# Row maxima of an attention kernel turned on TensorE in half precision instead of single

## Chip, cores and metric

The kernel runs on one core of a Trainium2 chip. The metric is the device time of one execution in microseconds; the median of several executions counts.

## What is computed

Two layers, each an attention block with a compressive memory (A) followed by a gated MLP (B), on 2048 rows of 640. Cut to what the change touches, the attention is, for each of 32 heads of 20 columns and each of 4 segments of 512 rows:

```python
x = x + A(layernorm(x))
    logits = einsum("bhqd,bhkd->bhqk", qs, ks) * scale + mask     # within a segment, causal
    p = softmax(logits, axis=-1)
    a_dot = einsum("bhqk,bhkd->bhqd", p, vs)
    a_mem = (phi(qs) @ M) / (phi(qs) @ z + 1e-6)                  # memory of the segments before
    o = g * a_mem + (1.0 - g) * a_dot
    M, z = M + phi(ks).T @ vs, z + phi(ks).sum()
x = x + B(layernorm(x))
```

The softmax needs the maximum of each row of logits; the change concerns how the kernel brings these maxima to where they are subtracted.

## The kernel before

Each layer has three phases: attention (`phase1a`), the MLP's input (`phase1b`) and its spatial product and output (`phase2`). The change lies in attention, which runs 64 **pairs** of heads (16 pairs in each of 4 segments) one after the other. Each pair takes three **steps**, numbered t; the first step of pair n has t = 3n, and `n, c = divmod(t, 3)` gives the step's number c within the pair. Numbers are held as sums of two half-precision parts, so most products are three matmuls.

A pair's scores are computed twice. `by_queries` (line 881) lays them out with queries on the partitions, two pairs ahead (LM = 2): each step writes one or two tiles of 128 queries for both heads into the PSUM tile mp, and DVE reduces them along the keys (line 899). The widths of a step, over both heads, are 1024 for c = 0, 768 and 256 for c = 1, and 512 for c = 2. The eight columns of maxima (two heads, four query tiles) go into the first columns of an SBUF tile mxs, of which there are two. `by_keys` (line 860) computes the scores again with keys on the partitions, which is the form that the product with the values needs. There the maxima have to vary along the columns, so they enter as two extra contraction rows of the query operand qk, rows 60 and 61 of each head's 64. ACT takes the exponential (line 877). The masks of both forms are small matmuls (line 845).

`maxes` (line 917) turns the maxima: a single-precision matmul of mxs with the identity writes them as rows into a PSUM tile mtp (line 922, 64 columns of weights, two passes in the profile); ACT scales it into the first half-precision part (line 924); DVE makes the remainder (line 926); two DMAs on SP's queue write the two parts into the rows of qk for both heads (line 928). They are needed by the pair's first `by_keys`, three steps after the step in which they are turned.

The PSUM tile mtp comes from a pool of a single buffer (apm, tag "ms"). It shares it with the reads of the memory (`read`, line 766, tile num, with the DVE part at lines 790 to 794), with its updates (`update`, line 799, tile mup, DVE part at line 814), and, once, with the scales of the other weights (`other_scales`). Reads and updates are issued near the end of steps with c = 1, and their DVE parts one step later.

The order of PE's instructions is written out by hand in `run` (line 977): what a step emits in turn is what PE runs in turn. A step emits `by_queries`, `by_keys`, in steps with c = 0 also `maxes`, then work postponed from earlier steps (`later`), the products with the values (`pvs`, line 930, one head at c = 2 and the other at c = 0), and then the dense work of the phase up to the mark t + 0.8 (`until`): projections of queries, keys and values (lines 665 and 725) and, late in the phase, the output projection (line 697). The updates of the memory (`half`) follow, and at last the rest up to t + 1, memory reads among it. Other engines' order follows from the program's order and a planner's estimate of when each instruction is ready. `behind(DVE)` holds an instruction back until the step's reduction has been issued. ACT splits probabilities into two parts with POOL (`cast`, lines 912 and 914). `fetch` (line 836) loads queries and keys of a pair four steps before `by_queries` needs them.

Of the kernel before, what the change touches and what calls it, by code (L numbers as in the profile page):

```python
# [8 lines left out]
F32 = mybir.dt.float32  # L9
F32R = mybir.dt.float32r  # L10
F16 = mybir.dt.float16
# [3 lines left out]
ALU = mybir.AluOpType  # L15
# [14 lines left out]
MS = 2.0 ** 14  # L30
# [184 lines left out]
def other_scales(g, stage, pool, psum, tag):  # L215

    nc = g.nc
    last = None
    for i, w in enumerate((g.wo, *g.wi, g.wu)):
        width = D if w.cols == D else w.cols // 2  # L220
        j = 0
        for k in range(w.nk):
            n = min(128, w.dram.shape[0] - 128 * k)
            for c in range(0, w.cols, width):
                t = stage.tile([128, D], F32, tag="bg", name="wmst")[:n, :width]
                nc.sync.dma_start(t, w.dram[k * 128:k * 128 + n, w.c0 + c:w.c0 + c + width])
                if last is not None:
                    nc.vector.tensor_reduce(*last, AX.X, ALU.max, apply_absolute_value=True)
                last = g.wap[:n, i, j:j + 1], t
                yield True  # L230
                j += 1
    nc.vector.tensor_reduce(*last, AX.X, ALU.max, apply_absolute_value=True)
    yield False
    nc.vector.tensor_reduce(g.wam[:, 3:7], g.wap, AX.X, ALU.max)
    pow2_scales(g, pool, psum, tag, g.wam, 3, 4)
    nc.vector.tensor_scalar(g.yw, g.pw[:, 0:1], g.pw[:, 3:4], 2.0 ** -19, ALU.mult, ALU.mult)
    nc.vector.tensor_scalar(g.sc[:, 8:10], g.pw[:, 4:6], 2.0 ** -24, None, ALU.mult)
# [322 lines left out]
DVE, ACT = mybir.EngineType.DVE, mybir.EngineType.Activation  # L560


class Attention:
# [41 lines left out]
    def setup(self, ctx):  # L605
        g, nc, tc = self.g, self.nc, self.tc
        pool = lambda n, b, **k: ctx.enter_context(tc.tile_pool(name=n, bufs=b, reuse_waits="tile", **k))
        sk, self.p3, self.pl2, self.pr = pool("ak", 1), pool("a3", 2), pool("al2", 2), pool("amr", 1)
        av, self.u4, self.u2, self.u1 = pool("av", 1), pool("au4", 4), pool("au2", 2), pool("au1", 1)
        self.e2, self.e1, ax = pool("ae2", 2), pool("ae1", 1), [pool(f"ax{i}", 1) for i in range(2)]  # L610
        self.pl1, self.bg = pool("al1", 1), pool("abg", 2)
        self.pd = pool("apd", 2, space=PSUM)
        self.px = pool("apx", 1, space=PSUM)
        self.pm = pool("apm", 1, space=PSUM)
        self.pe = pool("ape", 1, space=PSUM)
        self.po = pool("apo", 1, space=PSUM)
        self.qk = [sk.tile([128, 2, L], F16, name=f"qk{i}") for i in range(self.NQK)]
        self.vs = [p.tile([128, 4, H, 2 * DH + 1], F16, name=f"vs{i}") for i, p in enumerate((av, sk))]
        for t in self.vs:
            nc.gpsimd.memset(t[:, :, :, DH:DH + 1], 1.0)  # L620
        self.xt = [p.tile([128, 2, KD, L], F16, name=f"xt{i}") for i, p in enumerate(ax)]
        self.mxs = [sk.tile([128, 64], F32, name=f"mxs{i}") for i in range(2)]
        for t in self.mxs:
            nc.gpsimd.memset(t, 0.0)
        self.mst = [self.u1.tile([128, NU, 8, DH + 1], F32, name=f"mst{i}") for i in range(2)]

# [254 lines left out]
    def by_queries(self, m, c):  # L881

        g, nc = self.g, self.nc
        if not 0 <= m < self.N:
            return
        todo = []
        q2, k2 = self.qk[m % self.NQK][:, 0], self.qk[m % self.NQK][:, 1]
        mp = self.px.tile([128, 2, 512], F32, tag="mp", name="mp")
        mw, red = 0, []
        for i in QCH[c]:  # L890
            w = 128 * i + 128
            todo.append((mp, mw, w, q2, 60, slice(w - 128, w), k2, slice(0, w), "q", mw + w - 128))
            red.append((i, mw, w))
            mw += w
        self.emit(todo)
        if c == 0:
            self.mx[m] = self.mxs[m % 2][:, :8].rearrange("p (h t) -> p h t", h=2)
        for i, o, w in red:
            e = nc.vector.tensor_reduce(self.mx[m][:, :, i], mp[:, :, o:o + w], AX.X, ALU.max)  # L899
        self.lead.append(e)  # L900
        if c == 2:
            pass

    def cast(self, n, h):
# [9 lines left out]
            (nc.gpsimd if h == 0 or n < self.N - self.TAIL else nc.vector).tensor_tensor(PL[:, c], P[:, h, c], PH[:, c], ALU.subtract)  # L914
        self.P[n, h] = (PH, PL)

    def maxes(self, n):

        g, nc = self.g, self.nc
        del self.mx[n]  # L920
        tp = self.pm.tile([128, 512], F32, tag="ms", name="mtp")[:, :128]
        nc.tensor.matmul(tp[:64], self.mxs[n % 2], g.ident, start=True, stop=True)
        mr = self.pr.tile([8, 2, 128], F16, tag="mr", name="mr")
        nc.scalar.mul(mr[:, 0], tp[:8], -1.0 / MS)
        with self.behind(DVE):
            nc.vector.scalar_tensor_tensor(mr[:, 1], tp[:8], -1.0 / MS, mr[:, 0], ALU.mult, ALU.subtract)
        for i in range(2):
            nc.sync.dma_start(self.qk[n % self.NQK][60 + i:125 + i:64, 0].rearrange("h (t c) -> h t c", t=4), mr[:, i])

    def pvs(self, n, h, s, m, h0):  # L930
        nc = self.nc
# [45 lines left out]
    def run(self, nseg=NSEG):  # L977
        pairs = [(s, m, h0) for s in range(nseg) for m in range(NU) for h0 in UH[m][::2]]
        N = self.N = len(pairs)
# [44 lines left out]
        for s in range(nseg):  # L1024
# [4 lines left out]
            for c in seq:  # L1029
                beg = G * s - LEAD + span * acc / tot  # L1030
                if c == "v":
                    t, w = next(vt), V
# [5 lines left out]
                elif c == "p":  # L1038
                    t, w = next(pt), V
# [3 lines left out]
                else:  # L1043
                    m, w = int(c), U
# [20 lines left out]
        def background():  # L1065

            g = self.g
            yield 6
            if not g.wo.made:
                for i, _ in enumerate(other_scales(g, self.bg, self.pl1, self.pm, "ms")):  # L1070
                    yield 6 + 1.2 * i if _ else 53
            yield 54
            for j, (w, width) in enumerate(((g.wo, D), (g.wi[1], FHH))):
                w.tiles(g.top[j])
                for i, _ in enumerate(w.load(self.bg, width, "bg")):
                    yield 55 + 1.3 * (6 * j + i)

        for _ in early():
            pass
        streams = [[next(it), i, it] for i, it in enumerate((fills(), background(), dense(), reads()))]  # L1080

        def until(t):
            while streams:
                e = min(streams)
                if e[0] >= t:
                    return
                e[0] = next(e[2], None)
                if e[0] is None:
                    streams.remove(e)

        for t in range(-LEAD, END):
            self.now = t
            f, c = divmod(t + self.LF, 3)
            if c == 0 and 0 <= f + self.LM < N:
                self.fetch(f + self.LM)
            p, r = divmod(t - self.LV - 2, 3)
            if r == 0 and 0 <= p < N:
                self.combine(p, *pairs[p])
            n, c = divmod(t, 3)
            self.lead = []  # L1100
            self.by_queries(n + self.LM, c)
            self.by_keys(n, c)
            if c == 0 and 0 <= n - 1 + self.LM < N:
                self.maxes(n - 1 + self.LM)
            with self.behind(DVE):
                for f in self.later.pop(t, ()):
                    f()
            p, r = divmod(t - self.LV - 0, 3)
            if r == 0 and 0 <= p < N:
                for _ in self.pvs(p, 0, *pairs[p]):  # L1110
                    pass
            p, r = divmod(t - self.LV - 0, 3)
            if r == 0 and 0 <= p + 1 < N:
                with self.behind(ACT):
                    self.cast(p + 1, 0)
            p, r = divmod(t - self.LV - 1, 3)
            if r == 0 and 0 <= p < N:
                for _ in self.pvs(p, 1, *pairs[p]):
                    pass
            p, r = divmod(t - self.LV - 1, 3)  # L1120
            if r == 0 and 0 <= p + 1 < N:
                with self.behind(ACT):
                    self.cast(p + 1, 1)
            with self.behind(DVE):
                until(t + .8)
            for f in self.half.pop(t, ()):
                f()
            with self.behind(DVE):
                until(t + 1)
        assert not self.half  # L1130
# [73 lines left out]
```

## Time and profile before

| | us |
|---|---|
| median of three runs | 2349.11 (2349.03 to 2351.12) |
| the profiled execution | 2352.33 |
| its span, first to last instruction | 2350.6 |

Mean granted TensorE clock over the span: 0.985 of full speed. In the profile PE is TensorE's matmuls and PEld its weight loads, DVE is VectorE, ACT ScalarE, POOL GpSimd, SP the queue that issues the DMAs. A name such as L899 is line 899 of the kernel, `out<-in` are the tiles that an instruction writes and reads, and `<-` behind an idle time names what ended it.

### The profile page before, as it was taken

The numbers are of one execution on the slowest core, as the hardware profiler recorded it, in microseconds if no ns is written. First come the engines' busy times: TensorE is split into PE (matmuls) and PEld (weight loads), VectorE is DVE, ScalarE is ACT, GpSimd is POOL, SyncE is SP. The second block draws the span as 40 slices with busy tenths as digits, with TensorE's granted clock in tenths as the row PEclk, the third lists the DMA queues.
The fourth block names the chain that finished last, engine by engine and source line by source line (L and its number), as shares of the span: only waits on it lengthen the run. The fifth ranks groups of instructions, "written<-read, shape, count | busy, mean of one in ns | idle before, by whom it ended". The sixth has DMA issues, their size and how long they took to land. (4 is left out here: it accounts for less than half of the span.)

```text
span 2350.6 us, 53268 instructions
## 1 busy us (share of the span) xinstructions
PE 2207.0 (94%) x21834; PEld 1321.6 (56%) x21834; DVE 1391.3 (59%) x2705; ACT 1160.5 (49%) x1440; POOL 984.5 (42%) x980
## 2 busy tenths in 40 slices
PE   5898898999999989999988999989989999999998
PEld 3455555666555545555555556556665555555554
DVE  7788877777545545444327787777764544444331
ACT  4688788888522321111127988878872322112110
POOL 2487888999411000000015888899981100000000
PEclk9999899999999999999999999999999999999999
DMA  6665654345643697775534363453464338766661
GB/s 171 153 175 146 160 156 117 88 126 131 187 113 94 170 264 164 174 173 145 131 89 109 104 139 85 109 117 95 119 172 109 94 103 213 171 175 151 161 140 50
DMA packets 504884, 325.59 MB, mean 139 GB/s; under 512 B 410672, under 2 KB 445616, under 8 KB 499520
## 3 DMA queue, kind: packets, MB, share of 16 engines
q1 hardware_dynamic: 504640, 322.20, 53.9%
q8 instruction: 171, 2.80, 0.5%
q14 instruction: 73, 0.60, 0.1%
HBM read 148.42 MB, written 85.61 MB: 100 GB/s over the span
## 5 line engine op out<-in xcount | busy, mean ns | idle before, releaser
L914 POOL TENSOR_TENSOR PL<-P,PH 128x640 f16<-128x640 f32 x504 | 705.7, 1421 | 113.6 <-ACT PH L912 97.8
L899 DVE TENSOR_REDUCE mxs<-mp 128x2 f32<-128x1024 f32 (+3 forms) x512 | 409.0, 819 | 203.1 <-PE mp L845 199.5
L424 PE MATMUL gp<-zh,wt 128*128 128x432 f16 x2048 | 465.1, 347 | 9.5 <-DMA wt<-wn 9.5
L424 PEld LDWEIGHTS <-wt 128*128 128x128 f16 x3072 | 301.4, 98 | 270.1 <-DMA wt<-wn 10.4
L877 ACT ACTIVATE P<-es,sc 128x1024 f32<-128x1024 f32 (+1 forms) x384 | 370.9, 966 | 124.0 <-PE es L845 119.7
L912 ACT CAST PH<-P 128x1280 f16<-128x1280 f32 x256 | 320.0, 1250 | 10.4 <-PE pv L942 2.6
L439 POOL MEMSET un<- 128x64 f16 x32 | 5.0, 155 | 680.9 <-DMA ut<-un 656.2
L341 PEld LDWEIGHTS <-th 128*128 128x128 f16 x1920 | 187.8, 98 | 166.6 <-issue 3.8
L424 PE MATMUL gp<-zl,wt 128*128 128x432 f16 x1024 | 272.2, 348 | 0.0
L252 POOL TENSOR_TENSOR lnrs<-lnve,mhalf 128x1 f32<-128x1 f32 x96 | 59.7, 631 | 407.9 <-DVE lnve L251 400.6
L427 ACT ACTIVATE u<-gp,bsp,un 128x864 f32<-128x864 f32 x32 | 34.2, 1068 | 358.4 <-PE gp L424 356.7
L401 DVE TENSOR_REDUCE am<-wr 128x1 f32<-128x2048 f32 x32 | 73.2, 2286 | 213.4 <-DMA wr<-in_B_w_sp_dram 213.4
L854 PEld LDWEIGHTS <-qk 60*128 60x128 f16 (+1 forms) x2048 | 86.7, 94 | 185.6 <-issue 133.5
L453 PE MATMUL cyp<-wuh,ut 128*128 128x320 f16 (+1 forms) x896 | 166.7, 303 | 8.9 <-DMA ut<-un 8.9
L665 PE MATMUL vps<-wvh,xt 128*128 128x320 f16 x640 | 156.7, 312 | 19.0 <-DVE relu L754 8.5
L453 PEld LDWEIGHTS <-ut 128*128 128x128 f16 (+1 forms) x1344 | 132.8, 99 | 66.5 <-DMA ut<-un 10.5
L942 PE MATMUL pv<-vs,PH 128*128 128x41 f16 x2560 | 167.3, 182 | 0.6 <-DVE ab L958 0.6
L942 PE MATMUL pv<-vs,PL 128*128 128x41 f16 x2560 | 163.9, 181 | 2.0 <-POOL PL L914 1.9
L411 ACT ACTIVATE wn<-wr,ivw 128x1024 f16<-128x1024 f32 x64 | 71.9, 1144 | 185.3 <-DVE ivw L406 100.2
L854 PE MATMUL es<-qk 64*128 64x512 f16 (+3 forms) x1024 | 134.9, 300 | 28.1 <-ACT P L877 23.6
L942 PEld LDWEIGHTS <-PH 128*128 128x128 f16 x2560 | 140.7, 96 | 28.2 <-issue 21.2
L854 PE MATMUL mp<-qk 60*128 60x512 f16 (+3 forms) x1024 | 138.1, 307 | 16.8 <-DVE mxs L899 12.7
(185 smaller groups left out, 4123.7 us busy)
## 6 DMA issues: line engine op xcount, KB each, us to landing
wr<-in_B_w_sp_dram SPq DMA_DIRECT2D x32, 1024.0 KB
qk<-st SPq DMA_DIRECT2D x256, 120.0 KB
z<-z SPq DMA_DIRECT2D x32, 432.0 KB
cz<-z SPq DMA_DIRECT2D x32, 432.0 KB
xt<-in_A_x_dram SPq DMA_DIRECT2D x32, 320.0 KB
st<-qhl SPq DMA_DIRECT2D x40, 256.0 KB
st<-khl SPq DMA_DIRECT2D x40, 256.0 KB
x<-x SPq DMA_DIRECT2D x32, 320.0 KB
```

Source lines behind the costliest of these rows:

```text
L341: nc.tensor.matmul(zp[:, n, :FHH], a[:, k, :], b[:, k, c:c + FHH], start=(k == 0 and j == 0), stop=(k == KD - 1 and j == 2))
L401: nc.vector.tensor_reduce(am, wr, AX.X, ALU.max, apply_absolute_value=True)
L411: nc.scalar.activation(hl[:, 0], wr[:, c], AF.Identity, scale=ivw)
L424: nc.tensor.matmul(gp[:, n, :FHH], wt[:, k // 8, a, k % 8, :], b[:, k, n * FHH:(n + 1) * FHH], start=(k == 0 and j == 0), stop=(k == NT - ...
L453: nc.tensor.matmul(yp[:, n, :320], a[:kn[k], k, :], b[:kn[k], k, n * 320:(n + 1) * 320], start=(k == 0 and j == 0), stop=(k == KO - 1 and ...
L665: nc.tensor.matmul(ps, a[:, k, c], b[:, k, n * 320:(n + 1) * 320], start=(i == 0), stop=(i == 14))
L854: nc.tensor.matmul(out[:, h, o:o + w], a[r, ac], b[r, bc], start=o == 0, stop=False, skip_group_check=True)
L877: self.lead.append(nc.scalar.activation(P[:, :, 512 * c:512 * c + ew], es[:, :, :ew], AF.Exp, scale=g.esc))
L899: e = nc.vector.tensor_reduce(self.mx[m][:, :, i], mp[:, :, o:o + w], AX.X, ALU.max)
L912: nc.scalar.copy(PH, P[:, h])
L914: (nc.gpsimd if h == 0 or n < self.N - self.TAIL else nc.vector).tensor_tensor(PL[:, c], P[:, h, c], PH[:, c], ALU.subtract)
L942: nc.tensor.matmul(pv[:, i, h, :], x[:, c:c + 128], v[:, j, h0 + h, :], start=(j == 0 and x is PH), stop=(j == i and x is PL), skip_group_ ...
```

## The change

The maxima go into a single-precision tile mx of its own. At the end of the pair's third step (c = 2) the new function `split` runs on DVE: it scales the eight columns into a corner of the PSUM tile that the turn will use, copies them from there in half precision, and subtracts to get the remainder; both parts lie side by side in a half-precision tile of 128 columns (mhs), of which 16 are used and the others stay zero. `maxes` is moved from the front of the following step (c = 0), right behind `by_keys`, to its end, behind `until(t + .8)` and the updates. It is one half-precision matmul with the identity; ACT copies 16 rows out at once, and the two DMAs write one head each instead of one part each. The remainder is no longer formed after the turn. `mr` has two buffers instead of one. The PSUM buffer "ms" is held from `split` to ACT's copy, so the scales of the other weights move from step 53 to 52.

```diff
     def setup(self, ctx):
-        sk, self.p3, self.pl2, self.pr = pool("ak", 1), pool("a3", 2), pool("al2", 2), pool("amr", 1)
+        sk, self.p3, self.pl2 = pool("ak", 1), pool("a3", 2), pool("al2", 2)
...
-        self.mxs = [sk.tile([128, 64], F32, name=f"mxs{i}") for i in range(2)]
-        for t in self.mxs:
+        self.mhs = [sk.tile([128, 128], F16, name=f"mhs{i}") for i in range(2)]
+        for t in self.mhs:
             nc.gpsimd.memset(t, 0.0)
...
         if c == 0:
-            self.mx[m] = self.mxs[m % 2][:, :8].rearrange("p (h t) -> p h t", h=2)
+            self.mx[m] = self.pl2.tile([128, 2, 4], F32, tag="mx", name="mx")
...
+    def split(self, m):
+
+        nc = self.nc
+        mx = self.mx.pop(m)
+        mh = self.mhs[m % 2][:, :16].rearrange("p (h i t) -> p h i t", h=2, i=2)
+        tp = self.pm.tile([128, 512], F32, tag="ms", name="mtp")
+        self.tp = tp[:, :128]
+        ms = tp[:, 256:264].rearrange("p (h t) -> p h t", h=2)
+        nc.vector.tensor_scalar(ms, mx, -1.0 / MS, None, ALU.mult)
+        nc.vector.tensor_copy(mh[:, :, 0], ms)
+        nc.vector.tensor_tensor(mh[:, :, 1], ms, mh[:, :, 0], ALU.subtract)
+
     def maxes(self, n):
 
         g, nc = self.g, self.nc
-        del self.mx[n]
-        tp = self.pm.tile([128, 512], F32, tag="ms", name="mtp")[:, :128]
-        nc.tensor.matmul(tp[:64], self.mxs[n % 2], g.ident, start=True, stop=True)
-        mr = self.pr.tile([8, 2, 128], F16, tag="mr", name="mr")
-        nc.scalar.mul(mr[:, 0], tp[:8], -1.0 / MS)
-        with self.behind(DVE):
-            nc.vector.scalar_tensor_tensor(mr[:, 1], tp[:8], -1.0 / MS, mr[:, 0], ALU.mult, ALU.subtract)
-        for i in range(2):
-            nc.sync.dma_start(self.qk[n % self.NQK][60 + i:125 + i:64, 0].rearrange("h (t c) -> h t c", t=4), mr[:, i])
+        tp = self.tp
+        nc.tensor.matmul(tp, self.mhs[n % 2], g.ident16, start=True, stop=True)
+        mr = self.pl2.tile([16, 128], F16, tag="mr", name="mr")
+        nc.scalar.copy(mr, tp[:16])
+        for h in range(2):
+            r = 64 * h + 60
+            nc.sync.dma_start(self.qk[n % self.NQK][r:r + 2, 0].rearrange("i (t c) -> i t c", t=4), mr[8 * h:8 * h + 8])
...
-                    yield 6 + 1.2 * i if _ else 53
+                    yield 6 + 1.2 * i if _ else 52
...
             self.by_keys(n, c)
-            if c == 0 and 0 <= n - 1 + self.LM < N:
-                self.maxes(n - 1 + self.LM)
             with self.behind(DVE):
                 for f in self.later.pop(t, ()):
                     f()
+            if c == 2 and 0 <= n + self.LM < N:
+                self.split(n + self.LM)
...
             for f in self.half.pop(t, ()):
                 f()
+            if c == 0 and 0 <= n - 1 + self.LM < N:
+                self.maxes(n - 1 + self.LM)
             with self.behind(DVE):
                 until(t + 1)
```

## Rows read from the trace of the kernel before

**Rows 1.** The page, part 1: busy us (share of the span) and instructions of each engine.

```profile
PE 2207.0 (94%) x21834; PEld 1321.6 (56%) x21834; DVE 1391.3 (59%) x2705; ACT 1160.5 (49%) x1440; POOL 984.5 (42%) x980
```

**Rows 2.** Busy time by stretch: length, PE, PEld, DVE, ACT, POOL, PEclk, DMA share, GB/s.

```profile
420.00:592.00 172.00, 167.49 (x2627) 109.91 (x2626) 129.17 (x260) 141.03 (x174) 160.54 (x151) 1.00 0.44 115
500.00:560.00 60.00, 59.08 (x937) 38.51 (x936) 46.09 (x95) 50.25 (x63) 57.75 (x56) 1.00 0.45 121
```

**Rows 3.** Line 854, whole run: what ended PE's and PEld's idle time (us, times).

```profile
  DVE mxs L899: 48.0, 80
  ACT P L877: 23.6, 35
  DMA qk<-mr: 8.2, 6
```

**Rows 4.** Timeline of PE, 513.5 to 526.9 us: start, length, engine, line, operation, tiles.

```profile
513.97 0.43 PE L922 MATMUL mtp<-ident,mxs 128*64 128x128 f32 x2
...
521.12 0.22 PE L845 MATMUL es<-eye,stepk 64*128 64x64 f16 x4
521.28 0.43 PE L922 MATMUL mtp<-ident,mxs 128*64 128x128 f32 x2
521.64 0.20 PE L942 MATMUL pv<-vs,PH 128*128 128x41 f16 x1
...
526.42 0.22 PE L845 MATMUL es<-eye,stepk 64*128 64x64 f16 x4
526.57 0.19 PE L942 MATMUL pv<-vs,PH 128*128 128x41 f16 x1
```

**Rows 5.** Timeline of PE: a run of update matmuls, first and last; last of 20 pv.

```profile
305.79 0.24 PE L808 MATMUL mup<-vs,pk 128*128 128x168 f16 x1
...
306.65 0.24 PE L810 MATMUL mup<-vs,pk 128*128 128x168 f16 x1
...
522.13 0.18 PE L942 MATMUL pv<-vs,PL 128*128 128x41 f16 x1
```

**Rows 6.** Tile num, whole run: who waited for it (us, times).

```profile
  PEld mtp L922: 8.8, 10
```

**Rows 7.** Tile mr, whole run: duration in ns min/median/max, first and last start in us.

```profile
L924 ACT ACTIVATE mr<-mtp x128: 246/249/268, 74.6 to 1747.4; 8x128 f16<-8x128 f32 x128
L926 DVE SCALAR_TENSOR_TENSOR mr<-mtp,mr x128: 226/269/280, 75.4 to 1748.2; 8x128 f16<-8x128 f32 x128
```

**Rows 8.** DVE, 500 to 560 us by line; then line 899's idle time, 420 to 592.

```profile
L953 DVE TENSOR_TENSOR rs<-pv,iomg 128x8 f32<-128x8 f32 x8 | 1.3, 163 | 0.1
...
  PE mp L845: 36.0, 42
```

**Rows 9.** DVE parts of the memory's reads (tile num) and updates (mup), whole run.

```profile
L790 DVE SCALAR_TENSOR_TENSOR den<-num,sc,gate x36: 210/232/236, 199.3 to 1724.7; 128x24 f32<-128x24 f32 x30, 128x8 f32<-128x8 f32 x6
...
L814 DVE TENSOR_TENSOR mst<-mup,bmask x30: 299/315/325, 65.8 to 1615.6; 128x168 f32<-128x168 f32 x18, 128x147 f32<-128x147 f32 x12
```

**Rows 10.** Timeline of all engines, 513.5 to 525 us.

```profile
516.02 0.39 PE L854 MATMUL mp<-qk 60*128 60x384 f16 x4
...
520.91 0.38 PE L854 MATMUL es<-qk 64*128 64x512 f16 x2
...
522.46 0.25 ACT L924 ACTIVATE mr<-mtp 8x128 f16<-8x128 f32 x1
...
523.11 0.39 PE L854 MATMUL mp<-qk 60*128 60x384 f16 x4
...
523.77 0.58 ACT L739 ACTIVATE khl<-kps 128x512 f16<-128x512 f32 x1
...
524.12 0.38 PE L781 MATMUL num<-mst,phq 128*128 128x126 f32 x2
```

**Rows 11.** The chain that ended last, 1700 to 1760 us: start, length, what.

```profile
1714.45 2.50 DMA qk<-mr
...
1730.30 7.62 DMA qk<-mr
```

## The prediction, made before the changed kernel was run

> **What bounds the kernel now.** I read the page's totals first, then the busy time by stage, then who waits for whom, and last the timeline around one hand-over of the row maxima. PE is busy for 94% of the span [rows 1]. The edit lives in the two attention phases alone, so their stages count. In the late stage of the first one PE is busy 167.49 of 172 us, with POOL next at 160.54, then ACT at 141.03 and DVE at 129.17; in the densest 60 us POOL has 57.75 and PE 59.08 [rows 2]. PE is the bound there, but POOL follows it closely.
>
> The waits say the same. Over the whole run the query and key matmuls of line 854 waited 48.0 us for the reductions of the scores (DVE), 23.6 us in 35 places for the exponentials (ACT), and 8.2 us for the maxima's DMA [rows 3]; some of it is counted twice, for the weight load and its matmul. One turn of the maxima follows the last by 7.3 us there (513.97 to 521.28 [rows 4]); 64 such pairs make a phase of some 470 us, and there are two. Against that the waits are little. So what is taken off PE's own queue there should shorten the run, apart from the places where another engine ends the step anyway.
>
> **PE: the turn of the maxima.** There is one turn for each of the 64 pairs of heads and two layers, 128 in all. The last mask matmuls of a step are followed by the two-pass single-precision turn, and the first pv matmul starts 0.52 us after the masks did (521.12 to 521.64). In a step without the turn the same distance is 0.15 us (526.42 to 526.57) [rows 4]. I take the turn as 0.36 us of PE's queue. Removed: 128 x 0.36 = 46.1 us.
>
> The new turn is one half-precision matmul of 128 columns with 128x128 weights, between others of that array shape. Below it lie the pv matmuls of 41 columns, each with its own weights, at 26 ns apiece (19 from 521.64 to 522.13 [rows 4, 5]); above it the update matmuls of 160 to 168 columns, 11 of them from 305.79 to 306.65, so 78 ns each [rows 5]. Between these by columns, 128 give about 0.06 us: 128 x 0.06 = 7.7 us added. Net: 38.4 us, with 36 to 43 from the two ends. The Trainium skill (TensorE: Matmul & The Clock Gate, Back-to-back issue gap) gives about 81 ns for a sustained pair of weight load and matmul at 128 columns. By it the net would be an estimated 35.7 us; the rows with more columns at 78 ns speak for the smaller price.
>
> **The wait in front of the turn.** Today the turn also waits for its PSUM buffer, which the read-outs of the memory still hold: 8.8 us in 10 places [rows 6]. After the change DVE itself writes that buffer first, behind its own read-outs, and PE comes most of two steps later. This wait goes, but where DVE was late the next reduction is late too, so I count half: 4.4 us gained.
>
> **DVE.** Removed: one scalar_tensor_tensor of 269 ns, which today also has to wait for ACT [rows 7]. Added: three small operations on 128 x 8 elements, two of them with a PSUM operand read and one written. The nearest row reads 128x8 from PSUM at 163 ns [rows 8]; three make 0.49 us. A DVE write into PSUM is not shown; between the 163 ns and the 269 ns of the removed one, I take the near row. DVE thus gets 0.22 us more a pair. It falls into the third step, whose reduction is the shortest. In the stage of 420 to 592 us DVE stood idle 36.0 us before its reductions, waiting for PE [rows 8]; that is about 1.5 us for each of its 23 pairs (172 / 7.3). I cost it at nothing. Without that cover it would be 128 x 0.22 = 28 us.
>
> **ACT and SP.** The copy stays one short instruction (249 ns today [rows 7]; 16 partitions instead of 8, same columns), and the two DMAs keep their bytes. Their place moves: the matmul goes from the front of the step, at 513.97 for one pair [rows 4], to its end, about 515.7, as the next step begins at 516.02 [rows 10]; 1.7 us later. On ACT the exponentials of the next step can't come before PE has passed the turn anyway, so a copy that waits holds up no one but a cast, and behind it POOL's differences, which a pair's products need a whole pair later. On SP, the stacking and fetching DMAs behind the two issues start later; queries and keys are fetched four steps ahead, which hides it. POOL's queue is passed by nothing.
>
> Two things are late next. First, the PSUM buffer: it has one copy, and the memory reads and updates, at the end of the step after, need it back from ACT. There are 36 reads and 30 updates [rows 9]. Today ACT takes its part 1.18 us after the turn (521.28 to 522.46). With that lag from about 522.8, 0.3 ahead of the next step at 523.11, and 0.25 for itself, the copy ends at 524.23, where the read started at 524.12 [rows 4, 10]. That is 0.11 us late: 66 x 0.11 = 7 us lost. If ACT takes the copy at once nothing is lost; if it first finishes something else it is more (a rival). Second, the maxima's rows must land before the scores of two to three steps later. With the turn at 515.7, the issue at about 517.1 and 2.50 us to land [rows 11] they land at 519.6; the scores start at 520.91 [rows 10], or 0.3 earlier after the change. It holds with about 1 us to spare, but near the end of the second phase they took 7.62 us behind other traffic [rows 11]. Today such places cost 8.2 us [rows 3]; I take a good third of that on top, 3 us. One-off: the scales of the other weights move from step 53 to 52; the chain is the same, so nothing.
>
> **What the other engines keep.** At the 35 ACT waits the saved 0.30 us may simply make the wait longer: 35 x 0.30 = 10.5 us. ACT is partly fed by the same PE, so I take half, 5 us. POOL has 2.25 us free in the 60 densest us, where eight pairs would save 2.5; over the late stage it has 11.5 us free against 23 x 0.30 = 6.9 [rows 2]. It can't be filled without a gap: I take off 4 us for both layers.
>
> **Sum.** 38.4 + 4.4 - 5 - 4 - 7 - 3 = 24 us. Against the profiled execution's own 2352.33 us that is 2328; against the median of the three runs, 2349.11, which lies 3.2 us lower, it is **2325 us**.
>
> **Rivals.** (a) *All of it passes.* If ACT takes the copy at once and the waits are re-timed by PE itself, nothing is given back: 38.4 + 8.8 = 47 us, so 2302. For it: most waits of the score matmuls are for work that an earlier PE starts earlier, and the new place in the step spares a change of array shape. Against it: POOL's 57.75 of 60 us. 0.19.
>
> (b) *Nothing passes.* The step is held by POOL and ACT in turn (57.75 and 50.25 of 60 us), PE's queue shortens and its waits grow by as much: about 2349. Against it: PE itself is busy 59.08 of the 60 us, and POOL's 160.54 of 172 us leaves room. The same time would come out if the turn in half precision took as long as before, because its weights are not loaded behind the matmul ahead of it. 0.12.
>
> (c) *Slower: the PSUM buffer comes back late.* Place: the 66 reads and updates, which now follow the turn by one step instead of nearly two. Price: if ACT first does one more piece of the next step (a split of 0.58 us as at 523.77 [rows 10]), each waits 0.11 + 0.58 = 0.69 us, in all 45.5 us. With the other terms (38.4 + 4.4 - 5 - 4 - 3 = 30.8) that is 14.7 us slower: 2364. It decides from 30.8 / 66 = 0.47 us a wait on. For it: at 524.12 the read already comes close behind the release. Against it: the order of ACT follows the order of the program unless something is ready earlier, and the copy is emitted ahead of the next step's work. 0.08.
>
> **How the numbers follow.** The forecast, 2310 to 2340, has 0.61. A measurement of this kernel can tell 0.2%, or 4.7 us, from no change. Faster by more than that takes the forecast and (a): 0.80. Within it is (b): 0.12. Slower is (c): 0.08. The range goes from the end of (a), 2302, to just over (b), 2350; left out are (c) and what would lie beyond (a).
>
> **What would show it.** Right: PE has one matmul of some 60 ns slot for each pair near the end of the first step, the first pv follows the masks by 0.15 us in all steps, the attention phases are each about 12 us shorter, and POOL's share in 500 to 560 goes towards 99%. The wait of the turn for the memory's read-outs is gone, and reads and updates wait for ACT's copy by tenths of a microsecond. Wrong: those waits total over 30 us; or the score matmuls wait for the maxima's DMA in most pairs; or DVE's three small operations stand in front of a reduction that PE waits for, so that line 899's waits grow by tens of microseconds.

## The result, and the profile after

The changed kernel took 2355.8 us (median), the kernel before 2350.9 us beside it on the same chip: a ratio of 1.0019, 95% interval 1.0010 to 1.0028. The forecast was 2325 us. Below, a difference of two ratios is turned into microseconds with 2350, so the changed kernel is 4.5 us slower.

The page's part 1 of the changed kernel, and its busy time in the two stretches of [rows 2], with the same columns:

```profile
PE 2179.9 (92%) x21706; PEld 1310.1 (56%) x21706; DVE 1414.4 (60%) x2961; ACT 1159.8 (49%) x1440; POOL 985.8 (42%) x980
```

```profile
420.00:592.00 172.00, 161.34 (x2592) 106.97 (x2592) 132.41 (x309) 140.26 (x175) 160.48 (x152) 1.00 0.43 112
500.00:560.00 60.00, 56.16 (x914) 36.64 (x910) 46.27 (x109) 49.63 (x61) 55.68 (x54) 1.00 0.41 117
```

PE lost 27.1 us of busy time against [rows 1], and 6.15 of 172 us in the late stage against [rows 2]. But POOL, whose work for a pair is the same in both kernels, was busy 160.48 of these 172 us, and 160.54 before. Its share tells how fast pairs go by: just as fast as before. In the densest 60 us it fell, from 57.75 to 55.68, where the prediction had it rise towards 99%. What PE no longer works, it waits.

What PE did at two turns, from the timeline: first PE alone (start, length, engine, line, operation), then some lines of all engines.

```profile
501.29 0.38 PE L725 MATMUL kps<-xt,wkh 128*128 128x512 f16 x1
501.50 0.22 PE L933 MATMUL mtp<-ident,mhs 128*128 128x128 f16 x1
501.56 0.38 PE L725 MATMUL kps<-xt,wkh 128*128 128x512 f16 x1
```

```profile
528.38 0.16 DVE L925 TENSOR_SCALAR mtp<-mx 128x8 f32<-128x8 f32 x1
...
528.58 0.17 DVE L926 CAST mhs<-mtp 128x8 f16<-128x8 f32 x1
...
528.77 0.17 DVE L927 TENSOR_TENSOR mhs<-mtp,mhs 128x8 f16<-128x8 f32 x1
...
531.25 0.22 PE L933 MATMUL mtp<-ident,mhs 128*128 128x128 f16 x1
...
532.70 0.24 ACT L935 CAST mr<-mtp 16x128 f16<-16x128 f32 x1
...
532.99 0.49 PE L781 MATMUL num<-mst,phq 128*128 128x126 f32 x2 [0.42 <-ACT mr L935]
...
533.27 0.62 SPq L938 DMA_DIRECT2D qk<-mr  x1
```

The turn takes 0.06 us of PE's queue (501.50 to 501.56), as forecast. DVE's three operations take 0.16 to 0.17 us each, as forecast. At 532.99 a read of the memory waits for ACT to release the PSUM buffer, the wait of rival (c). The prediction had both attention phases about 12 us shorter. Between the first and the last exponential (line 877), the first phase of the profiled execution is 10.0 us longer (79.8 to 605.3 us before, 80.9 to 616.4 after) and the second 3.4 us shorter (1248.3 to 1756.5, 1260.5 to 1765.3). So where is the time? The waits of PE by what ended them, whole run (us, times, longest), first of the kernel before, then of the changed one:

```profile
PE es L854 <- ACT P L877: 23.6, 35, 2.3
PE mp L854 <- DVE mxs L899: 12.7, 21, 1.5
...
PE mtp L922 <- DVE gm L794: 7.5, 9, 2.8
...
PE es L854 <- DMA qk<-mr: 3.9, 3, 3.2
```

```profile
PE es L854 <- ACT P L877: 26.4, 41, 2.0
PE mp L854 <- DVE mx L899: 25.7, 30, 3.3
PE mtp L933 <- DVE mhs L927: 20.5, 21, 2.6
...
PE es L854 <- DMA qk<-mr: 5.2, 5, 1.9
...
PE mup L808 <- ACT mr L935: 1.8, 3, 1.3
...
PE num L781 <- ACT mr L935: 0.8, 2, 0.4
```

The reads and updates lost only 2.6 us (1.8 + 0.8). But PE waits 13.0 us more for the reductions of the scores, 20.5 us for the split where it waited 7.5 us for the reads of the memory, and 2.8 us more for the exponentials. Together that is 28.8 us, of the same size as what PE saved. It reads like a case against DVE. Counted as in [rows 3], with the weight loads of line 854, the waits for the reductions grew by 23.2 us, which the prediction had named as a sign of being wrong:

```profile
  DVE mx L899: 71.2, 90
```

The experiments say that it is only a part of the story.

### The profile page after: what moved, and what is told of

Its sections match the earlier page's. It is cut to its first block, busy times and chain, and to the rows that moved or that the text cites. A ratio compares the mean times of both kernels' runs of the same rounds, so it can differ in the third digit from the quotient of the medians.

```text
span 2357.0 us, 52982 instructions
## 1 busy us (share of the span) xinstructions
PE 2179.9 (92%) x21706; PEld 1310.1 (56%) x21706; DVE 1414.4 (60%) x2961; ACT 1159.8 (49%) x1440; POOL 985.8 (42%) x980
## 5 line engine op out<-in xcount | busy, mean ns | idle before, releaser
L899 DVE TENSOR_REDUCE mx<-mp 128x2 f32<-128x1024 f32 (+3 forms) x512 | 409.0, 820 | 175.2 <-PE mp L845 172.2
L453 PEld LDWEIGHTS <-ut 128*128 128x128 f16 (+1 forms) x1344 | 131.9, 98 | 67.2 <-DMA ut<-un 12.5
L854 PE MATMUL mp<-qk 60*128 60x512 f16 (+3 forms) x1024 | 138.3, 308 | 27.6 <-DVE mx L899 25.7
L341 PE MATMUL zp<-wi0h,th 128*128 128x432 f16 x640 | 148.8, 346 | 1.5 <-ACT z L354 1.1
```

Of the source, the lines that this page charges most:

```text
L341: nc.tensor.matmul(zp[:, n, :FHH], a[:, k, :], b[:, k, c:c + FHH], start=(k == 0 and j == 0), stop=(k == KD - 1 and j == 2))
L453: nc.tensor.matmul(yp[:, n, :320], a[:kn[k], k, :], b[:kn[k], k, n * 320:(n + 1) * 320], start=(k == 0 and j == 0), stop=(k == KO - 1 and ...
L854: nc.tensor.matmul(out[:, h, o:o + w], a[r, ac], b[r, bc], start=o == 0, stop=False, skip_group_check=True)
```

## The experiments

Ratios are to the kernel before, run on the same chip; less is faster.

### Place or split?

**e1_place**: the kernel before with its single-precision turn moved to the end of the step, all else as it was (ACT's and DVE's parts behind it).

```diff
-            if c == 0 and 0 <= n - 1 + self.LM < N:
-                self.maxes(n - 1 + self.LM)
             p, r = divmod(t - self.LV - 0, 3)
...
             for f in self.half.pop(t, ()):
                 f()
+            if c == 0 and 0 <= n - 1 + self.LM < N:
+                self.maxes(n - 1 + self.LM)
```

> The kernel before with one part of the change alone: the turn, still in single precision with its remainder formed behind it, stands at the end of its step instead of the front. Theory D (the changed kernel lost its gain on DVE, where the three operations ahead of the turn run late): nothing of that is here, so 2340 to 2355 us, no turn waits for a split. Rival P (the later place costs: the PSUM buffer comes back late from ACT and the maxima land late): slower than before by 10 us or more, 2360 to 2385, with waits of the memory's reads and updates for mr. Rival B (other engines hold the step, whatever PE does): 2349 to 2352, no difference.

Measured: 2427.9 us, ratio 1.0326 (1.0308 to 1.0344), slower than any of the three expectations. Its waits:

```profile
PE num L781 <- DVE mr L926: 22.8, 17, 3.3
...
PE es L854 <- DMA qk<-mr: 18.8, 12, 4.5
PE mup L808 <- DVE mr L926: 18.4, 20, 2.5
```

With the remainder still formed after the turn, reads and updates wait 41.2 us for DVE to release the PSUM buffer, and the maxima land late. The later place needs the split ahead of the turn.

**e2_turn_front**: the changed kernel with the turn back at the front, behind `by_keys` (the same lines moved the other way).

> The changed kernel with the place undone: the turn in half precision at the front of its step, right behind the scores. Theory D: the turn comes some 1.7 us earlier and meets DVE's split unfinished far more often; its waits grow from 20 us to 50 or more, and the time to 2365 to 2400 us. Rival P: the release and the landing come early again, 2330 to 2345 us. Rival B: as the changed kernel, 2353 to 2358.

Measured: 2398.9 us, 1.0205 (1.0189 to 1.0221). The split needs the later place as much: it is not ready.

```profile
PE mtp L933 <- DVE mhs L927: 82.1, 51, 3.9
```

**e6_twice**: the changed kernel with the three operations done twice, the second time into a spare tile.

```diff
+        mg = self.pl2.tile([128, 2, 2, 4], F16, tag="mg", name="mg")
+        nc.vector.tensor_scalar(ms, mx, -1.0 / MS, None, ALU.mult)
+        nc.vector.tensor_copy(mg[:, :, 0], ms)
+        nc.vector.tensor_tensor(mg[:, :, 1], ms, mg[:, :, 0], ALU.subtract)
```

> The changed kernel with DVE's three operations done twice, the second time into a spare tile that nobody reads. Theory D: another 0.5 us of DVE time a pair in the same place; the waits for DVE grow by 10 us or more, 2363 to 2380 us. Rival P: DVE is not what decides, 2353 to 2359. Rival B: also within 3 us of the changed kernel, as DVE is the least busy of the four engines.

Measured: 2397.0 us, 1.0201 (1.0183 to 1.0218), 42.8 us above the changed kernel and above the highest expectation.

```profile
PE mtp L937 <- DVE mg L931: 86.6, 63, 5.0
```

0.5 us more of DVE's work a pair cost 0.33 us a pair, which spoke for DVE as the cause. But the spare operations use the turn's PSUM buffer, so the turn waits for them too. A doubled cost shows what a second one costs, not what the first one did; the next runs took it out.

**e4_early**: the split without PSUM, in two operations from mx straight to mhs, right behind the reduction.

```diff
+        nc.vector.tensor_scalar(mh[:, :, 0], mx, -1.0 / MS, None, ALU.mult)
+        e = nc.vector.scalar_tensor_tensor(mh[:, :, 1], mx, -1.0 / MS, mh[:, :, 0], ALU.mult, ALU.subtract)
+        self.lead.append(e)
```

> The changed kernel with DVE's part made short and early: two operations from the SBUF maxima straight into the two halves (no PSUM, the PSUM buffer is taken at the turn), right behind the step's reduction and ahead of the postponed work. Theory D: the turn's wait for DVE goes from 20 us to under 3, the waits of the score matmuls for reductions fall back to about 13 us on PE, and the time is 2322 to 2338 us. Rival P: little changes, 2345 to 2355. Rival B: 2349 to 2355.

Measured: 2366.1 us, 1.0066 (1.0048 to 1.0084). The turn hardly waits any more for DVE's split (0.6 us), yet the kernel is 11 us slower than the changed one, and slower than all three expectations. Tile mhs of e4, then of the changed kernel (duration in ns, min/median/max):

```profile
L922 DVE TENSOR_SCALAR mhs<-mx x128: 153/468/1398, 75.4 to 1759.0; 128x8 f16<-128x8 f32 x128
L923 DVE SCALAR_TENSOR_TENSOR mhs<-mx,mhs x128: 152/432/1421, 75.6 to 1759.8; 128x8 f16<-128x8 f32 x128
```

```profile
L926 DVE CAST mhs<-mtp x128: 106/166/168, 75.1 to 1754.4; 128x8 f16<-128x8 f32 x128
L927 DVE TENSOR_TENSOR mhs<-mtp,mhs x128: 145/166/167, 75.3 to 1754.6; 128x8 f16<-128x8 f32 x128
```

From SBUF to SBUF the same eight columns take up to 1.4 us; through PSUM never more than 0.17. The timeline of e4 shows what they wait for, which is POOL:

```profile
542.12 2.76 POOL L914 TENSOR_TENSOR PL<-P,PH 128x640 f16<-128x640 f32 x2
543.61 1.29 DVE L922 TENSOR_SCALAR mhs<-mx 128x8 f16<-128x8 f32 x1
...
559.05 0.17 DVE L922 TENSOR_SCALAR mhs<-mx 128x8 f16<-128x8 f32 x1
559.25 0.17 DVE L923 SCALAR_TENSOR_TENSOR mhs<-mx,mhs 128x8 f16<-128x8 f32 x1
```

The first scaling ends at 544.90, 0.02 us after POOL's second instruction; the last two operations have no POOL instruction beside them. So it goes all through the run: each of the 148 operations of these two lines that took over 0.2 us ends 20 to 30 ns after a POOL instruction does, and the 77 with no POOL instruction beside them took 153 to 173 ns. The Trainium skill (SBUF — State Buffer, Who interferes with whom) says that a DVE scaling in its two-port mode contends with GpSimd for a port pair that the two share, where whoever issues first blocks the other for its whole instruction, and that a DVE operation with two SBUF inputs contends with a GpSimd instruction that reads SBUF. The trace agrees; whether the scaling ran in that mode, it does not tell.

### Without the split, and with it out of the turn's way

**e10_nosplit** is the changed kernel without the call of `split` and its three operations (mhs keeps its zeros); the turn takes its PSUM buffer itself, so the buffer is held from there on only. **e11_nosplit_front** is the same with the turn at the front.

```diff
-        tp = self.tp
+        tp = self.pm.tile([128, 512], F32, tag="ms", name="mtp")[:, :128]
...
-            if c == 2 and 0 <= n + self.LM < N:
-                self.split(n + self.LM)
```

> The changed kernel without DVE's part: the three operations of the split are left out, so the maxima are reduced but never subtracted; the turn runs on tiles of zeros, and takes its PSUM buffer itself. Theory D (DVE's three operations, late and ahead of the turn and of the next reductions, eat PE's gain): PE's gain comes out, 2315 to 2335 us, no wait of the turn over 9 us. Rival P (the later place of the turn eats it, by the buffer's late return and the late landing): 2345 to 2358 us. Rival B (other engines hold the step): 2347 to 2356.

> As the run without the split, with the turn back at the front of its step: the same part is left out. It prices the place alone, with neither DVE's part before the turn nor its remainder after it. Theory D: the place costs little, within 8 us of the run with the turn at the end, 2310 to 2335. Rival P: at least 12 us faster than that run. Rival B: both as before, 2347 to 2356.

Measured: e10 2353.6 us, 1.0011 (0.9996 to 1.0026); e11 2341.6 us, 0.9966 (0.9953 to 0.9978). Waits of e10, then of e11:

```profile
PE es L854 <- ACT P L877: 26.5, 47, 1.8
PE mp L854 <- DVE mx L899: 24.2, 35, 2.6
PE es L854 <- DMA qk<-mr: 12.9, 8, 3.8
```

```profile
PE es L854 <- ACT P L877: 32.8, 60, 1.3
PE mp L854 <- DVE mx L899: 16.8, 27, 1.5
...
PE es L854 <- DMA qk<-mr: 5.2, 3, 3.3
```

In e10 the 20.5 us of waits for the split are gone and the time hardly moves (1.9 us against the changed kernel): DVE's split as the one cause falls. The sign from above does not single out DVE either: counted as in [rows 3], e10 still waits 65.6 us for reductions. And even e11, with PE's whole saving, no split and no later place, gains 8.0 us of the 38.4.

**e13_mp** keeps the split, but in an unused corner of the scores' own PSUM tile, right behind the reduction; **e15_mp_front** is that with the turn at the front.

```diff
-        tp = self.pm.tile([128, 512], F32, tag="ms", name="mtp")
-        self.tp = tp[:, :128]
-        ms = tp[:, 256:264].rearrange("p (h t) -> p h t", h=2)
+        ms = self.mpt[:, :, 504:508]
```

> The changed kernel with the same three operations through PSUM, but their corner lies in the scores' own PSUM tile, so they can stand right behind the third step's reduction, ahead of all postponed work; the turn takes its buffer itself. Theory D: the turn's waits fall from 20 us to under 9, the scores of the next step wait up to 0.5 us more for their tile; 2325 to 2345 us. Rival P: 2350 to 2358. Rival B: 2347 to 2358.

> The three PSUM operations stand right behind the reduction, in a corner of the scores' PSUM tile, and the turn stands again ahead of the step's other products, where the kernel before has it. If the later place of the turn is what costs (e10 against e11 gave 12 us for it), the front place gives that back here too: 2340 to 2350 us. If DVE's three operations cost in their own right, the turn at the front waits for them as in e2, and the time is 2355 us or more.

Measured: e13 2356.4 us, 1.0025 (1.0014 to 1.0037); e15 2353.5 us, 1.0010 (1.0001 to 1.0020). Waits of e15:

```profile
PE mp L854 <- DVE mx L899: 23.4, 27, 3.9
PE mtp L932 <- DVE gm L794: 17.9, 15, 3.3
...
PE mp L854 <- DVE mhs L925: 7.3, 17, 0.8
```

The turn now waits for no split, and still nothing is gained: with the turn at the front, the split costs 10.3 us (e15 against e11). It delays the reductions (23.4 against 16.8 us), the release of the scores' tile (7.3 us), and DVE's part of the memory's reads, for which the turn waits 17.9 us (12.4 in e11, 7.5 in the kernel before). e15 fell between its two expectations, nearer to the second, but not in the way named there: the split costs by itself, through the DVE work behind it, and the turn does not wait for it as in e2.

e13 against e4 also prices the way through PSUM: both stand at the same place, and e13, with one operation more, is 9.6 us faster.

### The landing of the maxima

**e16_end_nodma**, **e17_front_nodma** and **e18_after_nodma** are e10, e11 and the changed kernel without the two DMAs that bring the turned maxima to their rows.

```diff
-        for h in range(2):
-            r = 64 * h + 60
-            nc.sync.dma_start(self.qk[n % self.NQK][r:r + 2, 0].rearrange("i (t c) -> i t c", t=4), mr[8 * h:8 * h + 8])
```

> e10 without the two DMAs that bring the turned maxima to their rows of the queries' tile (that part of the products is then missing, and the steps behind wait for no landing). If what the later place costs is the late landing of the maxima, this kernel and e17 come out within 3 us of each other. If the place costs through the order of PSUM buffers or the clock, this kernel stays 8 us or more above e17.

> e11 without the same two DMAs. If the landing of the maxima is hidden at the front place, this kernel is within 5 us of e11's 2341.6 us; if e11's 5.2 us of waits for the landing pass to the time, it is 5 us or more below.

> The changed kernel without the two DMAs of the turned maxima. e16 (no split, the turn at the end, no landing) took 2341.8 us. If the late landing carries the place's cost in the changed kernel too, and the split costs little by itself, this one takes 2340 to 2347 us. If the split takes the landing's place as what ends the waits, it takes 2350 us or more.

Measured: e16 2341.8 us, 0.9957 (0.9945 to 0.9968); e17 2341.5 us, 0.9961 (0.9947 to 0.9974); e18 2348.6 us, 0.9989 (0.9976 to 1.0002). Waits of e18:

```profile
PE es L854 <- ACT P L877: 26.1, 41, 1.8
PE mp L854 <- DVE mx L899: 25.9, 32, 3.2
PE mtp L933 <- DVE mhs L927: 22.0, 24, 2.6
```

At the front the DMAs cost nothing in time (e11 against e17), so having fewer DMAs is no gain in itself. At the end they cost 12.7 us (e10 against e16), and without them the two places are equal: the price of the later place is the landing. With the turn at the end, the four cases make a ledger (the split's entry includes that it holds the turn's PSUM buffer from then on):

| turn at the end | ratio | above e16, us |
|---|---|---|
| no split, no landing (e16) | 0.9957 | |
| split alone (e18) | 0.9989 | 7.5 |
| landing alone (e10) | 1.0011 | 12.7 |
| both (the changed kernel) | 1.0019 | 14.6 |

Each costs by itself. Together they cost 5.6 us less than their sum, about as much as the four intervals leave open. e18 fell between the two bounds that I had set. The intervals are 0.002 to 0.003 wide, so a ratio is sure to some 3 us, and a difference of two to some 5 us.

TensorE's granted clock, which e16's expectation named as a rival, is in the ledger as well. Its mean over the span, as a share of full speed (median of the executions), is 0.985 to 0.986 in the kernel before, 0.984 in the changed one, 0.982 in e10, e16 and e17, 0.985 in e11, 0.986 in e18 and 0.987 in e15. Over the 78 executions of the kernel before that ran beside e1 to e18, 0.001 less goes with 1.5 us more. By that estimate e16 loses some 6 us to e18 by the clock alone: at one clock the split alone would cost about 13 us instead of 7.5 (at the front 13 instead of 10.3), and e16 would gain about 15 us instead of 10.1. The landing's 12.7 us stand, as e10 and e16 have the same clock. At the front, e17's lower clock may hide 4 to 5 us that the landing costs there. Whether the clock falls because PE waits, or for another reason, no run here separates; it does not change that both split and landing cost, nor that most of PE's saving is kept.

### Slack in the other engines

If e16 gains only 10.1 us of 38.4, something holds the steps that is neither split nor landing. **l2_before** and **l2_front** are the kernel before and e11 with the split of the probabilities into two half-precision parts left out for the second half of its columns, so that ACT and POOL work less (the products take zeros there); **l23_before**, **l23_front** and **l23_after** (the changed kernel) have the reductions cut to 64 columns as well, so that DVE works less.

```diff
-        nc.scalar.copy(PH, P[:, h])
-        for c in (slice(0, 640), slice(640, 1280)):
+        nc.scalar.copy(PH[:, :640], P[:, h, :640])
+        for c in (slice(0, 640),):
...
-            e = nc.vector.tensor_reduce(self.mx[m][:, :, i], mp[:, :, o:o + w], AX.X, ALU.max)
+            e = nc.vector.tensor_reduce(self.mx[m][:, :, i], mp[:, :, o:o + 64], AX.X, ALU.max)
```

> The kernel before with less work on ACT and POOL: the split of the probabilities is left out for the second half of their columns (a tile of zeros stands in its place in the products), about 1.2 us of ACT and 2.8 us of POOL less a pair; PE's and DVE's work is the same. It is the base of the next run. Theory E (ACT and POOL hold the step, so PE's saving does not pass): 2300 to 2340 us, as those steps shorten to what PE needs. Theory F (DVE's loop of scores and reductions holds it): 2335 to 2350. Theory G (PE's own queue does, and the saving is not real): 2345 to 2351.

> The kernel with the half-precision turn at the front and no split (its 9.5 us gain stands against 38 us taken off PE), with the same half of the split of the probabilities left out. Theory E: with ACT and POOL out of the way the saving passes, 25 to 38 us under its base. Theory F: 5 to 15 us under it. Theory G: 5 to 12 us.

> As the base with less work on ACT and POOL, and the reductions cut to the first 64 columns of each tile, so DVE has some 2.5 us less a pair and the scores' tile comes free early; most keys are left out of the maxima. Base of the next run. Theory E: within 8 us of the other base. Theory F: 15 us or more under it. Theory G: within 5 us.

> The half-precision turn at the front and no split, with both cuts (half of the split of the probabilities and most of the reductions left out). With ACT, POOL and DVE all out of the way PE alone is left: theories E and F: 28 to 45 us under its base. Theory G (the saving on PE's queue is not real): 5 to 12 us under it.

> The changed kernel with the cuts of l23_front (ACT, POOL and DVE relieved). If the split and the later place cost in their own right, it stands 10 us or more above l23_front's 2284 us (2294 to 2312 us). If they cost only because DVE, ACT and POOL are the bound of the steps, it is within 5 us of 2284 us.

| | before | front, no split | changed |
|---|---|---|---|
| as they are | 1 | 0.9966 (e11) | 1.0019 |
| ACT and POOL relieved (l2) | 0.9931 (0.9908 to 0.9955) | 0.9821 (0.9807 to 0.9836) | not run |
| DVE relieved too (l23) | 0.9839 (0.9825 to 0.9854) | 0.9713 (0.9691 to 0.9734) | 0.9740 (0.9728 to 0.9753) |

In microseconds the medians are 2334.7 and 2310.4 for l2, and 2314.5, 2284.3 and 2290.0 for l23. Along each row, the cheap turn gains 8.0, 25.9 and 29.6 us; the changed kernel loses 4.5 us in the first row and gains 23.3 in the last. The same edit is worth what I forecast as soon as the other engines have room. Split and later place, 12.5 us in the first row (e11 to the changed kernel), cost 6.3 there: between the 10 and the 5 that I had set. Two things blur the rows. With ACT and POOL relieved DVE is relieved as well: its busy time falls from 1391.3 to 1361.1 us (the kernel before, l2_before). And by the medians l23_before is 20.2 us below l2_before, which is theory F's sign: DVE's reductions hold the step too, not ACT and POOL alone. The densest 60 us of l23_before, then of l23_after:

```profile
500.00:560.00 60.00, 59.39 (x962) 40.55 (x963) 28.21 (x93) 39.99 (x58) 35.13 (x38) 1.00 0.43 114
```

```profile
500.00:560.00 60.00, 59.38 (x1016) 41.37 (x1011) 30.35 (x112) 41.62 (x61) 35.63 (x39) 1.00 0.46 120
```

Here PE is the bound: it stays equally busy (59.39 and 59.38 us), does more matmuls in the same time (962 and 1016), and ACT and POOL get more done. Over the run, l23_after's matmuls of mp wait 2.0 us for the reductions, against 25.7 in the changed kernel.

### A cheaper turn without the rest

**e12_transpose**: the kernel before, with the turn as TensorE's transpose in place of a matmul with the identity. Place, tiles and DVE's part stay.

```diff
-        nc.tensor.matmul(tp[:64], self.mxs[n % 2], g.ident, start=True, stop=True)
+        nc.tensor.transpose(tp[:64], self.mxs[n % 2], g.ident)
```

> The kernel before with TensorE's own transpose of the single-precision maxima in place of the matmul with the identity; no other part of the change. If it takes one pass instead of two, PE's queue is shorter by about 0.16 to 0.2 us a pair at the same place, and DVE and ACT are untouched. Theory D: a gain on PE alone passes where DVE has no new work, 2325 to 2342 us. Rival P: the place is as before, so the same 2325 to 2342. Rival B: 2347 to 2353.

Measured: 2345.0 us, 0.9973 (0.9959 to 0.9987), 6.3 us faster than before and 10.8 faster than the changed kernel. PE around one turn:

```profile
510.93 0.22 PE L845 MATMUL es<-eye,stepk 64*128 64x64 f16 x4
511.08 0.30 PE L922 MATMUL mtp<-ident,mxs 128*64 128x128 f32 x1
511.22 0.18 PE L942 MATMUL pv<-vs,PH 128*128 128x41 f16 x1
```

It is one pass of single precision instead of two. The first pv follows the masks by 0.29 us, where it was 0.52 with the old turn and 0.15 without one [rows 4]; so its slot is 0.14 us, and 0.23 x 128 = 29 us are saved on PE's queue. 6.3 of them pass, about the share that e11 passes (8.0 of 38.4); the time fell between the expectations, nearer to theory B's. The Trainium skill (Perfetto Trace Analysis, Transposes) asks for transposes to be done as transposes and not as plain matmuls; this run agrees, with one pass against two.

## Why the prediction was wrong

- **PE's saving** was right: the slot of the new turn is 0.06 us. The Trainium skill (TensorE: Matmul & The Clock Gate, Back-to-back issue gap) gives about 81 ns for sustained pairs and, by its formula, about 56 ns for an isolated matmul of 128 columns; this trace agrees with the second.
- **"What the other engines keep"** is the step that failed: 5 us for ACT and 4 for POOL. With neither split nor landing (e16), 10.1 of 38.4 us pass, so about 28 are kept (some 24 at the clock of the kernel before). With ACT and POOL relieved 25.9 pass, with DVE relieved too 29.6. That is rival (b)'s mechanism, to which I gave 0.12. I argued from PE's 59.08 busy us of 60, but all of PE, POOL, ACT and DVE depend on each other in a step: PE writes scores, DVE (mp) or ACT (es) reads them, and only then may PE write the next ones, since each of these tiles has one buffer. A PE that is 98% busy there is not by that the bound: in l23_before, where the saving passes, its 59.39 us look almost the same. I priced only the 35 waits for exponentials that were visible; the runs showed that new ones appear (41 to 60 of them, and 27 to 35 for the reductions where there had been 21).
- **DVE "at nothing"** failed: 7.5 us for the split alone in this place (e18 against e16; about 13 at one clock), 10.3 at the front. The price of the operations was right, the cover was not. The 36.0 us that DVE stood idle before reductions [rows 8] was its turn to wait in that same loop, not room: what DVE does behind one reduction can delay the next.
- **The late landing, "3 us"**, was too small: 12.7 us alone, 7.0 on top of the split (the changed kernel against e18). I found 1 us to spare at one pair. The trace at another shows the copy 1.45 us after the turn (531.25 to 532.70) and the issue 0.57 us behind it.
- **The turn's wait** (+4.4) turned into another: 20.5 us for the split. Since e13 and e10 lack it and are no better than 1.0025 and 1.0011, it seems to cost little by itself and to stand where other waits would.
- **The PSUM buffer** (7 us, and rival (c) at 2364) came to 2.6 us of waits. The result lies toward (c), but not through its mechanism.

So of 38.4 us some 28 don't pass, and split and landing take 14.6: 4 us slower. What stays open is how the 28 us divide between ACT, POOL and DVE, since one cut relieved them together, whether split and landing really overlap, and why the clock differs.

## What to carry to other kernels

Where several engines hand one buffer back and forth, a high busy share does not make an engine the bound, and idle time before its partner's work need not be cover. Before pricing a saving on one engine, lighten the others in a throw-away kernel and see how much of it passes: here it was 8 us without and 30 us with. And a result that is moved later has to be followed to its landing in the densest place, not at one pair.

## What was not expected of the hardware

- DVE operations on 128 x 8 elements from SBUF to SBUF took 153 to 1421 ns (medians 468 and 432), while the same elements through PSUM took at most 168 to 171 ns. All the slow ones end 20 to 30 ns after a POOL instruction. The detour through PSUM, one operation more, is the cheaper way here (e13 against e4).
- A single-precision transpose of the maxima is one pass and 0.14 us of queue; the matmul with the identity is two passes and 0.37.
- The DMA issues of the turned maxima take 617 ns each in the changed kernel and 512 before (medians of 256), though the bytes are the same.
